# New positions for early loads and conversions, and identity products in PE's early gaps, in a three-phase fp32 attention-and-MLP kernel

## The chip, the cores and the metric

The kernel runs on one core of a Trainium2 chip. The metric is the device time of one execution in microseconds (us), reported as the median of several executions. Each execution also has a span (first to last instruction on the core) and a mean granted clock of PE, the matmul engine. The time was 1.8 to 2.2 us longer than the span in the executions that have both, 1.9 on average. The profile names the engines PE (matmul), PEld (PE's loading of the stationary operand), DVE (vector), ACT (scalar), POOL (general purpose) and SP, which here issues the loads and stores (DMA).

## The reference, cut to what matters

```python
kv  = np.einsum('bhsd,bhse->bhde', k, v)        # batch 8, heads 8, 576 tokens, 64
out = np.einsum('bhsd,bhde->bhse', q, kv)
x   = out / sqrt(mean(out*out, -1) + 1e-6) * g_norm      # -> 4608 x 512
h   = x @ w_in                                   # 512 -> 2048
g   = np.maximum(h, 0) + np.log1p(np.exp(-np.abs(h)))    # softplus
y   = g @ w_out                                  # 2048 -> 512
```

All is fp32, except that the weights arrive as float64 and are converted on the chip.

## The kernel before

Each fp32 operand is split into high and low parts, and a network product is three products of parts that accumulate in one bank. The hidden width is cut into 16 pieces in three phases of 4, 6 and 6; each phase passes over 12 blocks of 384 tokens, so there are 192 steps. A step is 12 products of the first layer and 9 of the second. Phase 0 also computes the attention, interleaved with its steps. Below, a *batch* is one of the eight of the attention.

The order of instructions on each engine is not written by hand. The program lists tasks with a duration, predecessors, buffers and a *position*, and a small planner in the program plays them through and emits them in the order of their planned start. Where several tasks are ready it takes the one with the lowest position:

```python
first = min(at for at, _ in options)
at, t = min(((at, t) for at, t in options if at <= first + self.SOON),
            key=lambda o: (o[1].pos, o[0]))
```

On the chip only the order survives, together with the waits for data and buffers.

```python
rings = dict(xv=2, gv=3, g=2, raw=2, ..., kvt=6, q=2, ..., h=2, o=2, tp=1, s0=1, s1=1, s2=1)
...
# K of two heads lands interleaved, in pieces of 64 floats; V lands in runs of 256 floats
for h in range(2):
    nc.sync.dma_start(out=x[:, h::2], in_=src[:, h])
...
nc.tensor.matmul(kv[:, i if tail else p], lhsT=l, rhs=r, ...)      # a "K and V group" is 4 of these; the profile counts each twice (x8)
...
# a part of a weight is made by PE, with the identity
nc.tensor.matmul(y, lhsT=ident_r, rhs=dst.tile[:, 0], start=True, stop=False)
nc.tensor.matmul(y, lhsT=minus_r, rhs=dst.tile[:, 1], start=False, stop=True)
```

The ring `kvt` has six places, one of which is held for a long time by another tile. A third pair of K and V tiles therefore has to wait until the first group of products has freed its places.

Of the kernel before, what the change touches and what calls it, by code (L numbers as in the profile page):

```python
# [18 lines left out]
P = 128  # L19
# [6 lines left out]
class Slot:  # L26


    def __init__(self, ring):
        self.ring, self.readers, self.place, self.tile = ring, 0, None, None  # L30
# [9 lines left out]
class Plan:  # L40
# [2 lines left out]


    HANDOVER = {"PE": 250, "ACT": 120, "DVE": 120, "POOL": 150, "SP": 0}
    SOON = 150

    def __init__(self, rings):
        self.tasks = []
        self.rings = rings  # L50

    def slot(self, ring):
        return Slot(ring)

    def add(self, engine, ns, run, after=(), pos=0.0, take=(), give=(), size=0, behind=None):
        t = Task(engine, ns, run, [a for a in after if a is not None], pos, list(take), list(give), size)
        for s in t.give:
            s.readers += 1
        self.tasks.append(t)
        t.behind = behind  # L60
        return t

    def order(self):
        waiting = {id(t): sum(1 for a in t.after) for t in self.tasks}
        users = {}
        for t in self.tasks:
            for a in t.after:
                users.setdefault(id(a), []).append(t)
        ready = {}
        for t in self.tasks:  # L70
            if not waiting[id(t)]:
                t.ready = 0
                ready.setdefault(t.engine, []).append(t)
        free = {r: [(0, i) for i in range(n)] for r, n in self.rings.items()}
        engine_free = {"PE": 0, "ACT": 0, "DVE": 0, "POOL": 0, "SP": 0}
        dma_free = 0
        last_read = {}
        done = []
        while len(done) < len(self.tasks):
            best = None  # L80
            for engine, tasks in ready.items():
                options = []
                for t in tasks:
                    at = max(engine_free[engine], t.ready)
                    if t.size:
                        at = max(at, dma_free - 2500)
                    for s in t.take:
                        if not free[s.ring]:
                            break
                        at = max(at, min(free[s.ring])[0])  # L90
                    else:
                        options.append((at, t))
                if not options:
                    continue
                first = min(at for at, _ in options)
                at, t = min(((at, t) for at, t in options if at <= first + self.SOON),
                            key=lambda o: (o[1].pos, o[0]))
                if best is None or at < best[0]:
                    best = (at, t)
            if best is None:  # L100
                raise RuntimeError("the plan is stuck at " + str([(e, t.pos, [s.ring for s in t.take if not free[s.ring]]) for e, ts in ready.items() for t in ts][:20]))
            at, t = best
            ready[t.engine].remove(t)
            for s in t.take:
                place = min(free[s.ring])
                free[s.ring].remove(place)
                s.place = place[1]
            t.start = at
            engine_free[t.engine] = at + t.ns
            t.end = at + t.ns + self.HANDOVER[t.engine]  # L110
            if t.size:
                dma_free = max(dma_free, at + t.ns) + t.size
                t.end = dma_free + 2000
            for s in t.give:
                s.readers -= 1
                last_read[id(s)] = max(last_read.get(id(s), 0), t.end)
                if not s.readers:
                    free[s.ring].append((last_read[id(s)], s.place))
            for u in users.get(id(t), ()):
                waiting[id(u)] -= 1  # L120
                if not waiting[id(u)]:
                    u.ready = max(a.end for a in u.after)
                    ready.setdefault(u.engine, []).append(u)
            done.append(t)
        return sorted(done, key=lambda t: t.start)
# [3 lines left out]
def kernel(  # L129
# [24 lines left out]
    nc = tc.nc  # L154
# [7 lines left out]
    TB = NT // P  # L162
    n_blocks = n_tokens // NT
    n_tiles = n_tokens // P
    PHASES = [range(0, 4), range(4, 10), range(10, 16)]
    PLACES = 8
    LAST = len(PHASES) - 1

    P0 = [-61.0, -9.7, -13.3, -2.2, -4.6, 5.5, -46.9, 0.2, -37.5, -33.8, -28.2, -10.7, -14.2, -13.7, 28.3, -2.7, 1.0, -9.0, 6.5, 7.0, 7.0, 20.0, -0.5, 2.5]
    CONVERT, FETCH, EARLY = P0[:8], P0[8:16], P0[16:]  # L170
    AT_ONCE = 2 * TB

# [6 lines left out]
    ident_r = const.tile([P, P], F32R, name="ident_r")  # L179
# [13 lines left out]
                 h=2, o=2, tp=1, s0=1, s1=1, s2=1)  # L193
    rings.update({f"w{i}_{c}": 1 for i in range(2) for c in range(PLACES)})
    PS = {"h", "o", "tp", "s0", "s1", "s2"}
    plan = Plan(rings)
    slot, add = plan.slot, plan.add

    def new(s, shape, dtype=F32):
        pool = ps if s.ring in PS else sb  # L200
        s.tile = pool.tile(shape, dtype, tag=f"{s.ring}_{s.place}", name=f"{s.ring}_{s.place}")
        return s.tile
# [8 lines left out]
    first_step = {}  # L211
# [163 lines left out]
    x_there = {}  # L375
# [143 lines left out]
            split(0, t, xg, a, pos + 0.5)  # L519

    def x_again(ph, t):
        pos = first_step[ph, t // TB] - 4 + 0.5 * (t % TB)
        xt = slot("xt")
        ld = add("SP", 350, lambda: nc.sync.dma_start(out=new(xt, [P, KD, P]).rearrange("p a t -> p (a t)"), in_=xd[t]),
                 [x_there[t]], pos - 1, [xt], [], 900, behind=first_step[ph, t // TB] - 5)
        split(ph, t, xt, ld, pos)


    part = {}
    scale_done = []  # L530
    mm1s = {}

    def step(s):
# [38 lines left out]
        for i in range(TB):  # L572
            last = c == cs[-1]
            a2 = add("PE", 700, lambda i=i: mm2(i), [a] + factors_done[1, c] + [mm2s.get(i)], s + 1.5,
                     [mine[i]] if c == cs[0] else [],
                     [gv] + ([w_out] if s == last_step[c] else []))
            mm2s[i] = a2
            if last:
                leave(ph, n * TB + i, mine[i], a2, s + 1.5)
# [3 lines left out]
    def leave(ph, t, bank, done, pos):  # L583

        ot = slot("xg" if ph == 0 else ("qT", "x", "q")[t % TB] if ph == LAST else "qT")
        if ph == 0:
            a = add("ACT", 600, lambda: nc.scalar.activation(new(ot, [P, d_model]), bank.tile, func=AF.Copy, scale=1.0 + E),
                    [done], pos, [ot], [bank])
        else:
            pt = slot("kvt")  # L590
            ld = add("SP", 350, lambda: nc.sync.dma_start(out=new(pt, [P, d_model]), in_=part[ph - 1, t][0]),
                     [part[ph - 1, t][1]], pos - 3, [pt], [], 900, behind=int(pos) - 4)
            a = add("DVE", 700, lambda: nc.vector.scalar_tensor_tensor(  # L593
                out=new(ot, [P, d_model]), in0=bank.tile, scalar=(scale if ph == LAST else 1.0 + E), in1=pt.tile,
                op0=ALU.mult, op1=ALU.add), [done, ld] + (scale_done if ph == LAST else []), pos, [ot], [bank, pt])
        dst = out[t * P:(t + 1) * P] if ph == LAST else dram.tile([P, d_model], F32, name=f"part{ph}_{t}")
        st = add("SP", 350, lambda: nc.sync.dma_start(out=dst, in_=ot.tile), [a], pos, [], [ot], 900)
        part[ph, t] = dst, st
# [24 lines left out]
    for x in kv_diag + tails:  # L623
        nc.vector.memset(x, 0.0)

    EACH = (first_step[PHASES[1][0]] - 9) / len(PHASES[1])
    for c in range(KF):
        for j in (2 * c, 2 * c + 1):
            if c in PHASES[0]:
                pos = CONVERT[j]  # L630
            elif c in PHASES[1]:
                pos = 5.0 + EACH * (c - PHASES[1][0] + 0.5 * (j % 2))
            else:
                pos = first_step[PHASES[2][0]] - 64.0 + 9 * (c - PHASES[2][0]) + 4.5 * (j % 2)
            weight(j, pos, FETCH[j] if c in PHASES[0] else pos)
    for b in range(B):
        kv_of(b)
# [3 lines left out]
    for ph in range(len(PHASES)):  # L641
        for n in range(n_blocks):
            for t in range(n * TB, (n + 1) * TB):
                if ph or t >= AT_ONCE:
                    x_again(ph, t)
# [4 lines left out]
    for t in plan.tasks:  # L650
        if t.behind is not None and t.behind >= 0:
            t.after.append(mm1s[t.behind])
    for t in plan.order():
        t.run()

# [29 lines left out]
```

## Time and profile before

| | kernel before |
|---|---|
| time, first set | 940.6 us median of 6 (939.86 to 943.16) |
| span of the profiled execution | 935.2 us (time 937.08 us) |
| PE idle time before the first network product | 16.8 us |
| first network product starts (timeline view) | 44.72 us |
| PE idle time from there to its last product | 0 |
| after PE's last product | 3.7 us |

The lines are in the prediction. Two habits help in reading them. First, the "time" of a kernel whose main engine is never idle after some moment is that moment, plus a constant; so only the moment is worth study. Second, a PE product's own duration tells whether the clock was up: eight identical attention products take about 2.05 us at the low clock and 0.89 at the full one. (The timeline view gives a group up to 0.2 us more than the chain does, since it includes the pipeline's end.)

### The profile page before, as it was taken

Reading aid. Unit: us, or ns where it says so; the run is one execution under the profiler, and the core shown is the slowest. Engines: PE = TensorE matmul, PEld = TensorE weight load, DVE = VectorE, ACT = ScalarE, POOL = GpSimd, SP = SyncE. Lnnn points to the kernel's source line nnn. Section 1 sums busy time; section 2 is a strip of 40 time slices with the busy share of each in tenths; the row PEclk is TensorE's granted clock in tenths of the full one; section 3 lists DMA queues with packets and bytes.
Section 4 is the critical chain, followed back from the end, with each engine's and each line's share of the span. In section 5 each row is a group of like instructions: output and inputs, shape, how many; then the busy total and the mean of one; then the engine's idle time right before and its main releaser. Section 6 shows DMA issues by size and latency. Waiting matters only on the chain.

```text
span 935.2 us, 13489 instructions
## 1 busy us (share of the span) xinstructions
PE 914.7 (98%) x4978; PEld 831.9 (89%) x4978; DVE 598.0 (64%) x1045; ACT 446.4 (48%) x871; POOL 66.2 (7%) x42
## 2 busy tenths in 40 slices
PE   4899999999999999999999999999999999999998
PEld 3799899999999899899989989899999999999997
DVE  7988876767777747676676665586455454444543
ACT  5877675756666635444344343374323333232331
POOL 0331212212222000000000000000000000000000
PEclk9999999999999999999999999999999999999999
DMA  9999677776554333434343332343232323322221
GB/s 248 251 261 265 198 219 219 221 210 192 172 193 141 119 124 125 146 124 134 137 134 106 122 139 100 135 145 102 102 102 102 102 102 102 101 91 75 91 82 69
DMA packets 148673, 135.63 MB, mean 145 GB/s; under 512 B 86400, under 2 KB 102784, under 8 KB 148608
## 3 DMA queue, kind: packets, MB, share of 16 engines
q1 hardware_dynamic: 148448, 134.78, 47.2%
q8 instruction: 39, 0.64, 0.3%
q14 instruction: 26, 0.21, 0.1%
q10 hardware_dynamic: 160, 0.00, 0.0%
HBM read 93.85 MB, written 40.89 MB: 144 GB/s over the span
## 4 chain that ended last, share of the span: by engine, by line
PE 96%; DMA 2%; SPq 0%; ACT 0%; issue 0%; DVE 0%; ACTq 0%
PE h L546 43%; PE s L553 43%; PE o L460 4%; PE o L484 3%; PE tp L500 2%; PE tp L478 2%; DMA q<-in_q_dram 1%; DMA kvt<-in_v_dram 1%; SPq L444 0%; PE s L484 0%; PE h L345 0%; PE h L344 0%; SPq L250 0%; DVE q L593 0%; ACT x L508 0%
## 5 line engine op out<-in xcount | busy, mean ns | idle before, releaser
L553 PE MATMUL s<-w,gv 128*128 128x512 f32 x1728 | 437.7, 396 | 0.0
L546 PE MATMUL h<-xv,w 128*128 128x384 f32 x2304 | 435.8, 337 | 0.0
L546 PEld LDWEIGHTS h<-xv,w 128*128 128x128 f32 x2304 | 405.4, 188 | 14.0 <-issue 0.2
L553 PEld LDWEIGHTS s<-w,gv 128*128 128x128 f32 x1728 | 318.3, 188 | 57.5 <-issue 0.3
L566 ACT ACTIVATE g<-h 128x384 f32<-128x384 f32 x192 | 94.3, 491 | 403.6 <-PE h L546 400.2
L557 DVE TENSOR_TENSOR gv<-g,gv 128x384 fp32r<-128x384 f32 x192 | 106.8, 556 | 173.3 <-ACT gv L568 172.9
L561 DVE SCALAR_TENSOR_TENSOR gv<-gv 128x384 fp32r<-128x384 f32 x192 | 107.0, 557 | 5.5
L568 ACT ACTIVATE gv<-g 128x384 fp32r<-128x384 f32 x192 | 100.7, 525 | 5.9 <-PE s L553 0.9
L401 DVE TENSOR_TENSOR xv<-xt,xv 128x512 fp32r<-128x512 f32 x102 | 70.2, 688 | 49.6 <-ACT xv L398 49.0
L492 POOL TENSOR_TENSOR r<-r,half 128x8 f32<-128x8 f32 x36 | 65.5, 1819 | 228.4 <-DVE r L489 228.4
L404 DVE SCALAR_TENSOR_TENSOR xv<-xv 128x512 fp32r<-128x512 f32 x108 | 74.5, 690 | 2.7
L398 ACT ACTIVATE xv<-xt 128x512 fp32r<-128x512 f32 x102 | 63.6, 623 | 11.0 <-DMA xt<-x 10.9
L460 PE MATMUL o<-kvt,kvt 128*128 128x128 f32 x256 | 36.9, 292 | 11.4 <-DMA kvt<-in_v_dram 10.9
L460 PEld LDWEIGHTS o<-kvt,kvt 128*128 128x128 f32 x256 | 35.1, 206 | 12.9 <-issue 12.0
L593 DVE SCALAR_TENSOR_TENSOR qT<-s,kvt 128x512 f32<-128x512 f32 x36 | 24.8, 688 | 28.5 <-PE s L553 25.9
L484 PE MATMUL o<-kv_diag,qT 128*128 128x128 f32 (+1 forms) x296 | 36.9, 276 | 0.0
L484 PEld LDWEIGHTS o<-kv_diag,qT 128*128 128x128 f32 (+1 forms) x296 | 34.6, 179 | 1.1 <-issue 0.8
L514 ACT ACTIVATE xg<-tp,g_col 128x512 f32<-128x512 f32 x36 | 24.7, 687 | 11.2 <-PE tp L500 11.0
L488 DVE TENSOR_REDUCE r<-x 128x8 f32<-128x512 f32 x36 | 24.6, 683 | 6.3 <-ACT x L508 6.0
L495 DVE TENSOR_TENSOR x<-o,r 128x512 f32<-128x512 f32 x33 | 22.7, 688 | 9.0 <-POOL r L492 8.6
L593 DVE SCALAR_TENSOR_TENSOR qT<-s,scale,kvt 128x512 f32<-128x512 f32 x12 | 9.0, 751 | 29.5 <-PE s L553 29.5
L503 ACT COPY qT<-tp 128x512 f32<-128x512 f32 x36 | 21.0, 583 | 12.7 <-PE tp L478 12.6
(66 smaller groups left out, 484.9 us busy)
## 6 DMA issues: line engine op xcount, KB each, us to landing
xt<-x SPq DMA_DIRECT2D x102, 256.0 KB, 3.3
kvt<-part SPq DMA_DIRECT2D x72, 256.0 KB, 4.4
x<-xg SPq DMA_DIRECT2D x36, 256.0 KB, 2.6
part<-xg SPq DMA_DIRECT2D x36, 256.0 KB, 2.5
part<-qT SPq DMA_DIRECT2D x36, 256.0 KB, 2.5
raw<-in_moe_w_in_dram SPq DMA_DIRECT2D x16, 512.0 KB, 5.2
raw<-in_moe_w_out_dram SPq DMA_DIRECT2D x16, 512.0 KB, 4.8
kvt<-in_k_dram SPq DMA_DIRECT2D x64, 128.0 KB, 4.0
```

The source lines that it names most:

```text
L398: nc.scalar.activation(cols(0, F32R), x.tile, func=AF.Copy, scale=DOWN)
L401: nc.vector.tensor_tensor(out=cols(1, F32R), in0=x.tile, in1=cols(0), op=ALU.subtract)
L404: nc.vector.scalar_tensor_tensor(out=cols(2, F32R), in0=cols(1), scalar=-RADIX, in1=cols(0), op0=ALU.mult, op1=ALU.add)
L460: nc.tensor.matmul(kv[:, i if tail else p], lhsT=l, rhs=r, start=(p == 0 and i == 0), stop=tail, skip_group_check=True)
L484: nc.tensor.matmul(pairs(y[r0:r0 + n], p), lhsT=qT.tile[:, p, r0:r0 + n], rhs=kv_diag[b % 2][:, p], start=(p == 0), stop=True, skip_group_ ...
L492: nc.gpsimd.tensor_tensor(out=r.tile, in0=r.tile, in1=half, op=ALU.pow)
L546: nc.tensor.matmul(hp, lhsT=w_in.tile[:, i, kd * P:(kd + 1) * P], rhs=xv.tile[:, i, kd], start=(m == 0), stop=(m == 3 * KD - 1))
L553: nc.tensor.matmul(mine[i].tile, lhsT=gv.tile[:, m, i * P:(i + 1) * P], rhs=w_out.tile[:, m], start=(c == cs[0] and m == 0), stop=(c == cs ...
L557: nc.vector.tensor_tensor(out=gv.tile[:, 1], in0=g.tile, in1=gv.tile.bitcast(F32)[:, 0], op=ALU.subtract)
L561: nc.vector.scalar_tensor_tensor(out=gv.tile[:, 2], in0=f32[:, 1], scalar=-RADIX, in1=f32[:, 0], op0=ALU.mult, op1=ALU.add)
L566: a = add("ACT", 490, lambda: nc.scalar.activation(new(g, [P, NT]), h.tile, func=AF.Softplus, scale=1.0 + E), [a], s, [g], [h])
L568: a = add("ACT", 530, lambda: nc.scalar.activation(new(gv, [P, 3, NT], F32R)[:, 0], g.tile, func=AF.Copy, scale=DOWN), [a], s, [gv])
```

## The change

The intent is to fill PE's early gaps with products of the identity whose results nobody reads, so that its clock stays up, and to replace hand-picked positions by ones found by playing the order through with varied landing times of the loads. The planner puts a filler wherever a 400 ns product ends before PE's next real task would start, from 4 us of planned time until the first network product. The diff, cut to its core (the bookkeeping of the planner's loop is left out):

```diff
@@ class Plan
+    BEGIN = 4000
...
+        self.spare = None
...
+                if engine == "PE" and self.spare and self.spare[-1].start is None:
+                    ring, run, ns, _ = self.spare
+                    begin = max(engine_free["PE"], self.BEGIN, min(free[ring])[0] if free[ring] else at)
+                    if begin + ns <= at:
+                        s = Slot(ring)
+                        at, t = begin, Task("PE", ns, lambda s=s: run(s), [], 0.0, [s], [s], 0)
+                        s.readers = 1
...
-    P0 = [-61.0, -9.7, -13.3, -2.2, -4.6, 5.5, -46.9, 0.2, -37.5, -33.8, -28.2, -10.7, -14.2, -13.7, 28.3, -2.7, 1.0, -9.0, 6.5, 7.0, 7.0, 20.0, -0.5, 2.5]
+    P0 = [-57.5, -0.2, -24.8, -1.2, -4.6, 5.5, -63.4, 1.2, -34.0, -33.3, -32.7, -11.2, -17.2, -25.2, 23.8, -3.7,
+          1.0, -9.5, 6.5, 7.0, 7.0, 24.5, -0.5, 2.5, 2.5, 8.5, -9.5, 5, 9, 67.5, 8]
     CONVERT, FETCH, EARLY = P0[:8], P0[8:16], P0[16:]
...
-        pos = first_step[ph, t // TB] - 4 + 0.5 * (t % TB)
+        pos = first_step[ph, t // TB] - EARLY[8] + 0.5 * (t % TB)          # conversion of reloaded x
-                 [x_there[t]], pos - 1, [xt], [], 900, behind=...)
+                 [x_there[t]], pos - EARLY[9], [xt], [], 900, behind=...)  # its reload
...
-                     [part[ph - 1, t][1]], pos - 3, [pt], [], 900, behind=...)
+                     [part[ph - 1, t][1]], pos - EARLY[10], [pt], [], 900, behind=...)
...
-    EACH = (first_step[PHASES[1][0]] - 9) / len(PHASES[1])
+    EACH = (first_step[PHASES[1][0]] - EARLY[12]) / len(PHASES[1])
...
-                pos = 5.0 + EACH * (c - PHASES[1][0] + 0.5 * (j % 2))
+                pos = EARLY[11] + EACH * (c - PHASES[1][0] + 0.5 * (j % 2))
...
-                pos = first_step[PHASES[2][0]] - 64.0 + 9 * (c - PHASES[2][0]) + 4.5 * (j % 2)
+                pos = first_step[PHASES[2][0]] - EARLY[13] + EARLY[14] * (c - PHASES[2][0]) + EARLY[14] / 2 * (j % 2)
...
+    def warm(s):
+        nc.tensor.matmul(new(s, [P, 4, P]), lhsT=ident_r, rhs=ident_r.unsqueeze(1).to_broadcast([P, 4, P]),
+                         start=True, stop=True)
+
+    plan.spare = ("h", warm, 400, mm1s[0])
```

More of the change, by code (lines that the diff above doesn't have):

```diff
@@ L77, in order @@
         last_read = {}
-        done = []
-        while len(done) < len(self.tasks):
+        done, left = [], len(self.tasks)
+        while left:
             best = None
@@ L102, in order @@
             at, t = best
-            ready[t.engine].remove(t)
+            if t in ready[t.engine]:
+                ready[t.engine].remove(t)
+                left -= 1
             for s in t.take:
@@ L521, in x_again @@
     def x_again(ph, t):
-        pos = first_step[ph, t // TB] - 4 + 0.5 * (t % TB)
+        pos = first_step[ph, t // TB] - EARLY[8] + 0.5 * (t % TB)
         xt = slot("xt")
         ld = add("SP", 350, lambda: nc.sync.dma_start(out=new(xt, [P, KD, P]).rearrange("p a t -> p (a t)"), in_=xd[t]),
-                 [x_there[t]], pos - 1, [xt], [], 900, behind=first_step[ph, t // TB] - 5)
+                 [x_there[t]], pos - EARLY[9], [xt], [], 900, behind=first_step[ph, t // TB] - 5)
         split(ph, t, xt, ld, pos)
@@ L591, in leave @@
             ld = add("SP", 350, lambda: nc.sync.dma_start(out=new(pt, [P, d_model]), in_=part[ph - 1, t][0]),
-                     [part[ph - 1, t][1]], pos - 3, [pt], [], 900, behind=int(pos) - 4)
+                     [part[ph - 1, t][1]], pos - EARLY[10], [pt], [], 900, behind=int(pos) - 4)
             a = add("DVE", 700, lambda: nc.vector.scalar_tensor_tensor(
```

## The prediction

> **What bounds the kernel now.** I read the page's busy shares first, then the windows view over the stages, then the chain that ended last.
>
> ```profile
> PE 914.7 (98%) x4978; PEld 831.9 (89%) x4978; DVE 598.0 (64%) x1045; ACT 446.4 (48%) x871; POOL 66.2 (7%) x42
> ```
>
> PE is busy 914.7 of 935.2 us, so 20.5 us is all the idle time there is. The windows view (start:end, length, then busy time of PE, PEld, DVE, ACT, POOL, granted clock, DMA share, GB/s) says where it lies:
>
> ```profile
> 0.00:8.70 8.70, 0.00 (x0) 0.01 (x1) 5.85 (x14) 4.78 (x8) 0.70 (x6) 1.00 0.75 211
> 8.70:20.60 11.90, 9.20 (x45) 8.21 (x45) 8.55 (x15) 6.38 (x13) 0.00 (x0) 0.86 1.18 272
> 20.60:44.70 24.10, 18.66 (x142) 15.70 (x143) 21.84 (x40) 20.45 (x39) 7.18 (x4) 1.00 1.15 254
> 44.70:330.00 285.30, 285.30 (x1773) 263.38 (x1772) 213.59 (x383) 188.94 (x368) 58.28 (x32) 1.00 0.69 199
> 330.00:931.60 601.60, 601.54 (x3024) 544.59 (x3022) 347.38 (x595) 225.85 (x445) 0.00 (x0) 1.00 0.33 111
> 931.60:935.20 3.60, 0.00 (x0) 0.00 (x0) 0.73 (x2) 0.00 (x0) 0.00 (x0) 0.81 0.58 219
> ```
>
> Before 44.7 us PE idles 44.7 - 9.20 - 18.66 = 16.8 us; after 931.6 us the last output leaves in 3.6 us; between them PE is never idle. Busy is not peak, so I also asked the chain between those two times whether any piece of it is stretched: grouped by kind, every product there costs the same (first product of the network 175 ns, second 231 ns, attention products 110 ns); the only longer pieces are one group of twelve at 2.33 and one at 2.21 us instead of 2.10, 0.34 us together. So after the first product of the network, which starts at 44.96 us in the chain, there is nothing to win: 931.55 - 44.96 = 886.6 us of pure PE work. The time is this start, plus 886.6, plus 3.6.
>
> What sets the start is read from the chain in order of time (start, length, what; cuts marked):
>
> ```profile
> 3.15 5.44 DMA kvt<-in_v_dram
> 8.58 0.14 issue
> 8.72 2.06 PE o L460 x8
> 10.78 0.02 issue
> 10.80 4.24 DMA kvt<-in_v_dram
> ...
> 17.25 1.98 PE o L460 x8
> ...
> 19.69 0.90 PE o L460 x8
> ...
> 29.87 4.57 DMA q<-in_q_dram
> 34.44 0.14 issue
> 34.58 0.64 PE tp L478 x4
> 35.22 0.02 issue
> 35.24 5.96 DMA q<-in_q_dram
> ```
>
> It is a ladder of loads: a product frees a buffer, the freed buffer lets the next load be issued, that load lands 4 to 6 us later. The loads are slow because the DMA engines are full: share 1.18 and 1.15 at 272 and 254 GB/s from 8.7 to 44.7 us. DVE (21.84 of 24.1) and ACT (20.45) are nearly full there as well.
>
> **What the Trainium skill says.** "TensorE: Matmul & The Clock Gate", Part 1 (the HAM clock gate): PE runs at half clock until about 3.4 us of sustained activity, and falls back after an idle window. The trace agrees in the durations: eight identical attention products took 2.06 us at 8.72 and 1.98 us at 17.25, but 0.90 at 19.69 and 0.89 everywhere later. Its clock column shows only the second of these (0.86 mean in that stage, and 0.50 between 16 and 18 us in a finer view), so for the first I believe the durations. The same page gives 427 ns cold and 216 ns warm for a product with 512 columns; the before trace has 230 ns warm for such a product (the pairs with the identity that divide a weight). "DMA: Bandwidth & Descriptors", Specifications: line rate needs 512 B or more per descriptor, and HBM gives a core about 358 GB/s. The page of the profile counts 86,400 of 148,673 packets under 512 B, which fits the early rate of 250 to 270 GB/s. In "Queues, rings and completion order" it has every DMA from one issuer share the same 16 engines: so reordering loads lets one land earlier only by making another later. The landing times here (4 to 6 us under load against 2.0 to 2.6 for the late stores) agree.
>
> **The change part by part.** The real work is the same: 939 PE rows before, and 980 after with 41 identity products of 512 columns added. All 41 stand ahead of the first network product, so none can cost anything later except by delaying that start.
>
> Comparing orders: the 37 PE rows of real work before the first network product are the same rows in the same order. The DVE order is the same for its first 83 rows; ACT's differs only in rows 6 to 9 (the squaring for the second weight waits until the first weight's overflow check is through). On the DMA queue, the first K and V loads move ahead of the second 512 KB weight load, and one K tail load moves behind the next two; from the thirteenth row to the eightieth that order is then unchanged. Nearly all the moved positions act past the first network product, on DVE and ACT conversions and reloads.
>
> 1. First K and V earlier. 512 KB less in front of them at 250 to 270 GB/s is 2.0 us: they should land near 6.7 instead of 8.6 us. The third V load is issued when the first products have freed its buffer (10.80 us, at the end of those products). With a start near 6.9 and 1.0 to 2.0 us of products, the buffer frees by 8 to 9 us; the queue reaches that load at about 9 us. So it is issued some 1.8 us earlier. But the engines are full, and the second weight's bytes now lie among them: I keep about half, 0.9 us.
> 2. Warm clock. Groups at 17.25 and the first ones before it cost 1.64 + 1.98 against 2 x 0.89 warm: 1.8 us of excess. The load of the fourth V lands at about 17.2 in any case if the DMA rate stays, so only the fourth group's own excess, 1.98 - 0.89 = 1.1 us, is on the path.
> 3. Cost of the fillers. Each about 0.23 us warm (0.43 cold, an estimate from the clock page): 6 cold ones from 1.6 us (the identity is ready at 1.57) end at 4.2, before any data. The other 35 are 35 x 0.23 = 8 us, against 16.8 - 8.7 = 8.1 us of measured idle time after the first data. So they fit only just, and not gap by gap: four stand before a transpose of q where the trace has 0.65 us of waiting, so 0.3 us may be added there, and two more sites may add as much. I charge 0.5 us, since a late transpose also delays the next q load.
> 4. Afterwards. There is no slack to win, so new positions of conversions and reloads can only lose or break even; that they were chosen for varying landings argues for zero. DVE has 213.6 of 285.3 us busy and ACT 188.9 up to 330 us, so room remains. A small wait somewhere, 0.2 us, is charged.
>
> Sum: -0.9 - 1.1 + 0.5 + 0.2 = -1.3 us in the profiled span. The timed runs (940.79 median) are 3.7 us longer than the profiled execution (937.08), and that difference cannot be read here. If part of it comes from landings which vary between runs, an order chosen for varied landings gets some back: I add -1.0 us as a guess. 940.8 - 1.3 - 1.0 = 938.5 us.
>
> **Rivals.** (a) DMA hides everything. The start at 44.96 us is set by the bytes ahead of the last needed q tile, and these are the same. For it: share above 1.1 throughout, and the unchanged order of loads from the thirteenth row on. Against it: the rungs of the ladder where a freed buffer issues the load (10.80, 28.17, 35.24 us). Then 940 to 941. (b) Fillers get in the way. PE keeps program order, so when data come earlier than planned the fillers stand in front of real products, and each costs 0.23 us or twice that if the clock stays low; with waits between fillers for one of the two banks they may cost more. Fully exposed, the 19 fillers behind the first batch's K and V products would be 4.4 us: 943 to 945. Against it: the gaps they were put in are mostly seen in the trace. (c) The whole ladder moves: each rung inherits the earlier buffer, and PE idle falls by 4 to 6 us. For it: four rungs pass through PE. Against it: full DMA, DVE and ACT. Then 935 to 936. (d) A new wait in the first stage past the start, because conversions of weights come later than the products that need them: PE would show idle time between 45 and 330 us. Then up to 945.
>
> **Range and chances.** Two per cent is 18.8 us, more than all the idle time before the start (16.8), of which 6 to 7 us is unavoidable first landing. So faster by over 2% is almost excluded. Slower by over 2% needs more than all 41 fillers exposed (41 x 0.23 = 9.4 us) plus a new stall. Rival (a) is the likeliest of the others, then (c), then (b). The range 934.8 to 942.0 covers (a) and (c) and half of (b).
>
> **What would show it.** Right: first attention products near 7 us; eight of them at 0.9 us each group from about 10 us on; the first network product at 43 to 44.5 us; no PE idle time between it and the last product; PE's busy time up by about 8 to 11 us while the idle time before the start falls by as much. Wrong: the start unchanged although PE is warm (a); transposes of q beginning later than the landing, behind identity products (b); a start before 42 us (c); a wait of PE on a weight's conversion after 45 us (d). If timed runs fall by much more than the profile's start moves, the gain came from the runs that no profile shows.

## The result, and the profile after

| set of runs | before, mean (runs) | changed, mean (runs) | ratio (95% interval) |
|---|---|---|---|
| first | 941.03 (6) | 938.97 (6) | 0.9978 (0.9965 to 0.9992) |
| second | 940.52 (11) | 939.38 (5) | 0.9990 (0.9975 to 1.0004) |
| fourth | 939.93 (11) | 939.89 (6) | 0.9998 (0.9979 to 1.0016) |

The result of the first set, which the prediction was about, is 938.95 us median (938.22 to 940.17) against 940.6. The second and fourth sets were run later, next to the experiments. The third set, on another chip, has experiments and the kernel before, but not the changed kernel. Over the three sets of the table the gain is between nothing and 2 us. A gain of about 1 us is likely, but only the first set's interval excludes that there is none.

The surprise is in the profile. The changed kernel's profiled execution has a span of 936.5 us, 1.3 us *longer* than the 935.2 of before, where the prediction's sum had it 1.3 us shorter. First the busy line of the page and the windows view (start:end, length, then busy time of PE, PEld, DVE, ACT, POOL, granted clock, DMA share, GB/s):

```profile
PE 925.1 (99%) x5019; PEld 837.3 (89%) x5019; DVE 601.5 (64%) x1045; ACT 449.3 (48%) x871; POOL 66.9 (7%) x42
```

```profile
0.00:8.70 8.70, 4.56 (x14) 3.32 (x15) 5.84 (x14) 3.64 (x6) 0.70 (x6) 1.00 0.77 224
8.70:20.60 11.90, 10.68 (x56) 7.89 (x55) 8.57 (x15) 7.53 (x15) 0.00 (x0) 1.00 1.17 272
20.60:44.70 24.10, 21.94 (x153) 17.28 (x152) 20.81 (x38) 19.64 (x38) 7.15 (x4) 1.00 0.95 238
44.70:330.00 285.30, 285.12 (x1774) 263.01 (x1773) 213.68 (x385) 188.99 (x368) 59.06 (x32) 1.00 0.69 200
```

PE is 10.4 us busier, and in the three early rows it has filled most of its idle time: 44.7 - 4.56 - 10.68 - 21.94 = 7.5 us are left of 16.8. DMA share and rate, the last two columns, hardly moved in the first two rows; in the third they fell from 1.15 to 0.95 and from 254 to 238 GB/s, so the engines are less full there than the prediction took them to be. The 0.18 us that are missing in the last row are a transpose that waited for DVE at 165.6 us. Now the chain that ended last, in order of time (start, length, what; L668 is the filler, L472 a K and V group):

```profile
2.61 4.32 DMA kvt<-in_v_dram
6.93 0.14 issue
7.06 2.05 PE o L472 x8
9.11 2.47 PE h L668 x7
11.58 0.89 PE o L472 x8
...
12.50 5.33 DMA kvt<-in_v_dram
17.83 0.04 issue
17.87 1.16 PE o L472 x8
...
19.49 0.91 PE o L472 x8
...
34.55 5.95 DMA raw<-in_moe_w_out_dram
...
45.86 2.09 PE h L558 x12
```

The first K and V did land earlier, as predicted (6.93 instead of 8.58 us). The fourth group ran at the full clock, 1.16 us instead of 1.98. The first batch's last group ended at 20.40 instead of 20.59. But the first network product starts later: 45.86 instead of 44.96 in this view (45.61 and 44.72 in the timeline). So the profile says that the change lost 0.9 us ahead of the start, while the timed runs say that it won. The loss lies between the end of the first batch's groups and the start: 25.5 us instead of 24.4. The chain passes there through the load of a second-layer weight, for which DVE waits (34.55); it does so in five of the eight traces that have the new order of loads with K in its old form, and in none of the four with the old order. Why that load binds there is not shown. The experiments are about this contradiction.

### The profile page after: what moved, and what is told of

It reads as the page before. It is cut to its first block, busy times and chain, and to the rows that moved or that the text cites. A ratio compares the mean times of both kernels' runs of the same rounds, so it can differ in the third digit from the quotient of the medians.

```text
span 936.5 us, 13571 instructions
## 1 busy us (share of the span) xinstructions
PE 925.1 (99%) x5019; PEld 837.3 (89%) x5019; DVE 601.5 (64%) x1045; ACT 449.3 (48%) x871; POOL 66.9 (7%) x42
## 2 busy tenths in 40 slices
DMA packets 148673, 135.63 MB, mean 145 GB/s; under 512 B 86400, under 2 KB 102784, under 8 KB 148608
## 4 chain that ended last, share of the span: by engine, by line
PE 95%; DMA 2%; DVE 1%; ACT 1%; issue 0%; SPq 0%; ACTq 0%
PE h L558 43%; PE s L565 42%; PE o L472 3%; PE o L496 3%; PE tp L512 2%; PE tp L490 1%; DMA kvt<-in_v_dram 1%; DMA raw<-in_moe_w_out_dram 1%; DMA part<-xg 0%; PE s L496 0%; PE h L668 0%; DVE xv L413 0%; PE h L357 0%; DVE xv L416 0%; SPq L456 0%
## 5 line engine op out<-in xcount | busy, mean ns | idle before, releaser
L413 DVE TENSOR_TENSOR xv<-xt,xv 128x512 fp32r<-128x512 f32 x102 | 70.1, 687 | 17.8 <-ACT xv L410 17.5
L472 PE MATMUL o<-kvt,kvt 128*128 128x128 f32 x256 | 35.0, 281 | 3.7 <-DMA kvt<-in_v_dram 3.7
L472 PEld LDWEIGHTS o<-kvt,kvt 128*128 128x128 f32 x256 | 33.4, 195 | 5.8 <-issue 3.2
```

The lines of the kernel that those rows point to most:

```text
L413: nc.vector.tensor_tensor(out=cols(1, F32R), in0=x.tile, in1=cols(0), op=ALU.subtract)
L472: nc.tensor.matmul(kv[:, i if tail else p], lhsT=l, rhs=r, start=(p == 0 and i == 0), stop=tail, skip_group_check=True)
```

## The experiments

Two theories were on the table. **W**: the identity products hold PE's clock up, and that is the whole gain; the first trace of the kernel before was an unusually quick execution. **P**: the new positions are the gain. For both I could keep the order of all real instructions fixed: with fillers switched off in the planner, the order of every engine's other instructions came out unchanged, for the new positions and for the old ones. So the change separates into two clean factors.

Below, *start* is the first network product in the timeline view, and *the batch ends* with the first batch's last K and V group. Each profile is one execution; the times are medians, and a mean is called one.

### The kernel before, again

No edit.

> The kernel before, unchanged, for a second trace and the spread of its runs. The first trace had a span of 935.2 us, while its timed runs (940.6 us median) must have spans near 938.7. If the first trace was a lucky execution, this one has a span of 937.5 to 940 and the first network product starts at 47 to 49 us instead of 44.96 with the work behind it still 886.6 us. Rival: the start is near 45 us again and the extra 3 us are waits of PE behind the start. Time ratio 1.000 within 0.1%.

Measured: 940.57 us median (939.86 to 941.51, 5 runs), ratio 1.000 (0.9985 to 1.0015), span of the trace 939.6 us. Its start is 48.87 us, 4.15 us later than in the first trace, and the work behind it is 887.1 us with 0.06 us of idle time, nearly as before (886.8). So the start alone differs between two executions of the same kernel. Two lines of PE's timeline (start, length, operation, and in brackets the idle time ahead) show one reason:

```profile
39.25 1.09 PE L478 MATMUL tp<-ident_r,q 128*128 128x128 f32 x4 [1.52 <-ACT qT L503]
40.13 1.91 PE L484 MATMUL o<-kv_diag,qT 128*128 128x128 f32 x8
```

The same eight products took 1.06 us in the first trace. The clock had fallen again, late in the start, after a few waits of 0.6 to 1.5 us. In this trace the first four groups were also slow, up to 22.17 us, where the first trace recovered at 19.7. The first trace was the lucky one: of the 36 later executions of the kernel before, the shortest span is 935.8 us.

### Identity products with the old positions

```diff
-    P0 = [-57.5, -0.2, -24.8, ... 2.5, 8.5, -9.5, 5, 9, 67.5, 8]
+    P0 = [-61.0, -9.7, -13.3, ... 4, 1, 3, 5.0, 9, 64.0, 9]     # the old values
```

> The old positions with the 41 identity products (every real instruction in the order of the kernel before). Theory W (the gain is the warm clock and the regular start it gives): 938.5 to 939.5 us, nearly all of the 1.7 us gain. Theory P (the gain is the positions): 940 to 942 us, no gain or a loss of up to 1 us from products standing in front of real work.

Measured: 939.57 us median (938.08 to 940.29, 5 runs), ratio 0.9990 (0.9975 to 1.0004), the same ratio as the whole change beside it; start 46.21, batch end 20.3 us. This is what W expects, though the interval alone does not exclude that nothing changed. With the later repeat below, the mean is 939.24 us in 11 runs against 940.22 in the 22 of the kernel before beside them: 1.0 us less, and by my working from these runs the 95% interval is about 0.2 to 1.8.

### The new positions without identity products

```diff
-    plan.spare = ("h", warm, 400, mm1s[0])
+    plan.spare = None
```

> The new positions without identity products (every real instruction in the order of the changed kernel). Theory W: 940 to 941 us, no gain; the first groups of attention products cold at about 2 us each. Theory P: 938 to 939.5 us, nearly all of the gain.

Measured: 940.76 us median (939.21 to 945.03, 6 runs), ratio 1.0007 (0.9988 to 1.0026). No gain is seen, which speaks against P, but the interval is wide enough to hide one of 1 us (and one run of 945.03 us widens it); the tiny products below settle it. The chain of its trace shows what the products had been doing:

```profile
10.46 2.06 PE o L472 x8
...
12.54 4.98 DMA kvt<-in_v_dram
...
17.57 2.08 PE o L472 x8
...
20.49 1.72 PE o L472 x8
```

Compare this with the chain of the changed kernel. Without fillers the second group starts 1.1 us earlier, as soon as its V has landed, but takes 2.06 us; with them it waits behind seven fillers and then takes 0.89. Both end at the same time (12.52 and 12.47), and the next load, which needs the freed buffer, is issued at 12.54 and 12.50 us. At that rung the fillers cost exactly what they bring. The gain comes after: the fourth group and the last one are fast, and the batch ends at 20.40 instead of 22.21 us. The recorded clock of this window (the third column from the end) reads 1.00 in both traces, although the groups differ by a factor of two. Without fillers:

```profile
8.70:20.60 11.90, 8.20 (x32) 6.84 (x31) 8.55 (x15) 6.63 (x14) 0.00 (x0) 1.00 1.18 268
```

### The changed kernel, again

No edit.

> The changed kernel, unchanged, for a second trace and the spread: 938.5 to 939.5 us, ratio 0.998 to before; span 936.4 to 938, first network product between 45 and 47 us, no PE idle time behind it. Its runs should scatter less than those of the kernel before (0.5 us rather than 1.2 us standard deviation).

Measured: 939.37 us median (937.97 to 940.48, 5 runs), ratio 0.9990 (0.9975 to 1.0004), span 938.6. The start is 47.19 us, slightly beyond what I expected, since the first V landed at 8.61 us in this execution instead of 6.93; the span is beyond it too (936.4 to 938), and behind the start PE idles 0.46 us where I expected none. The scatter of its runs is 0.84 us here (standard deviation) where I expected 0.5, against 1.22 for the kernel before.

### Tiny identity products

```diff
-        nc.tensor.matmul(new(s, [P, 4, P]), lhsT=ident_r, rhs=ident_r.unsqueeze(1).to_broadcast([P, 4, P]),
+        nc.tensor.matmul(new(s, [P, 4, P])[:, 0, :8], lhsT=ident_r, rhs=ident_r[:, :8],
```

> The changed kernel with each of the 41 identity products cut from 512 columns to 8: the same places, banks and waits, but hardly any array work. Theory W (only the activity of the array counts): the K and V groups run cold again at about 2.05 us, the recorded clock is below 1.0 in several runs, and the time is that of the positions alone, 940.2 to 941.2 us (ratio 0.9995 to 1.0010). Rival S (the extra instructions help in another way, by spacing or by the banks they take, or the new positions need them): 938.5 to 939.5 us, ratio 0.998 to 0.999.

Measured: 940.7 us median (940.16 to 942.87, 5 runs), ratio 1.0017 (1.0005 to 1.0030); so even a little slower than the kernel before of its set (939.41 mean), and beyond the ratio of 1.0010 that W allowed. The kernel of the same set with all fillers and six more (below) had a mean of 939.55, against 941.04 here. PE's timeline:

```profile
6.93 2.05 PE L472 MATMUL o<-kvt,kvt 128*128 128x128 f32 x8 [3.85 <-DMA kvt<-in_v_dram]
17.75 2.08 PE L472 MATMUL o<-kvt,kvt 128*128 128x128 f32 x8
```

All four groups are cold. The same 41 instructions in the same places, with the same banks and waits, do not warm the groups when they hardly use the array: it is the activity that counts. The rival that instructions help by spacing is out, and so is P: positions without activity bring no gain.

### Only the first 22 fillers, and only the last 19

```diff
+        warmed.append(s)
+        if len(warmed) > 22:        # the other kernel: <= 22
+            return
```

> The changed kernel with only the first 22 identity products, those ahead of the fifth K and V group of the first batch. Theory W1 (the early warm-up is the whole gain): K and V groups warm from the second on, 938.7 to 939.5 us. Theory W2 (the later 19 are needed against a fallback of the clock between 20 and 45 us): some runs with a recorded clock of 0.993 to 0.997 and times above 941, median 939.7 to 940.5.

> The changed kernel with only the last 19 identity products (from the first batch's last K and V group on). Theory W1: the first batch's groups cold as in the positions alone, its end at about 22.2 us instead of 20.4, median 940 to 941 us. Theory W2: the recorded clock stays at 0.998 to 1.0 and no run is over 941; median 939.3 to 940.

Measured: 940.39 us median (939.27 to 941.87, 5 runs) with the early ones, ratio 1.0011 (0.9999 to 1.0024); 940.82 (940.19 to 941.2, 5 runs) with the late ones, ratio 1.0015 (1.0001 to 1.0029). The kernel before of this set was at 939.41 mean, lower than in the other sets, so I read these by their traces. With the early ones alone the batch ends at 20.8 us, but then:

```profile
37.09 1.09 PE L490 MATMUL tp<-ident_r,q 128*128 128x128 f32 x4 [1.02 <-DMA q<-in_q_dram]
39.76 1.92 PE L496 MATMUL o<-kv_diag,qT 128*128 128x128 f32 x8
```

This is the fallback that the second trace of the kernel before also had; the start is 48.70 us. With the late ones alone three of the first four groups are cold (2.04, 2.05, 1.13 and 2.08 us), the batch ends at about 21.5 us, and the start is 46.97 us with no fallback behind 22 us. For the late ones W2 expected no run over 941 us; there were two (941.05 and 941.2). So W1 alone and W2 alone both look too little: in these two traces each half guards its own stretch. In time the two halves are 0.9 and 1.2 us slower than the full fillers of this set (939.55 mean), which is about the scatter of five runs.

### Twelve identity products ahead of the first group instead of six

```diff
-    BEGIN = 4000
+    BEGIN = 1600
```

> The changed kernel with six more identity products ahead of the first K and V group (12 instead of 6), so that PE is active from 1.6 us until about 6.9 us. If the first group ran cold only because PE idled from 4.5 to 7.1 us, it now runs in 0.9 to 1.2 us instead of 2.05, the seven products behind it in 1.7 us instead of 2.5, and the load which waits for the second group is issued 1.5 us earlier; time 937.5 to 939 us if the DMA lets it land earlier, 938.7 to 939.5 (no change) if the DMA rate binds.

Measured: 939.56 us median (937.85 to 940.65, 5 runs), ratio 1.0002 (0.9989 to 1.0014). The first group is warm now, as expected, and nothing comes of it:

```profile
7.74 1.13 PE L472 MATMUL o<-kvt,kvt 128*128 128x128 f32 x8 [0.64 <-DMA kvt<-in_v_dram]
18.09 1.16 PE L472 MATMUL o<-kvt,kvt 128*128 128x128 f32 x8 [1.37 <-DMA kvt<-in_v_dram]
```

The load ahead of the fourth group was not issued 1.5 us earlier, as I had expected, but at 12.58 us, as in the changed kernel (12.50). The second group could begin only at 11.01 us, when its loads had landed. By then the first two groups were done (12.14 us), and SP was still issuing the loads ahead of this one in its queue, until 12.48. PE's speed is no longer what sets this rung; the loads are.

### The whole change and the fillers alone, on another occasion

No new edits.

> The changed kernel once more, because the kernel before was itself 1.1 us faster on the chip of the last set (939.4 mean) than on the one before (940.5). If the gain is real on every chip, the ratio is 0.998 to 0.999 again; if on this chip the kernel before keeps its clock up by itself (recorded clocks of 0.996 to 0.998 and none of 0.993), the ratio is 0.999 to 1.0005 and its own runs are 938.5 to 939.5 us as on both occasions before.

> The old positions with the identity products, once more: as the changed kernel within 0.5 us (theory W: the products are the whole effect), 938.5 to 939.7 us; if the positions bring something that the first comparison hid, 0.7 us or more slower than the changed kernel of this set.

Measured: the changed kernel 939.78 us median (938.69 to 941.75, 6 runs), ratio 0.9998 (0.9979 to 1.0016); the fillers at the old positions 939.11 (938.71 to 939.74, 6 runs), ratio 0.9989 (0.9972 to 1.0006). The fillers alone do at least as well as the whole change in both sets. My reading that the kernel before would hold its clock here did not hold: it had runs from 937.68 to 943.72, the slowest at a recorded clock of 0.990 and the next at 0.993, and the ratio was near 1 all the same. The trace of the changed kernel shows that fillers are no guarantee. After a wait of 1.75 us for a load, its fourth group was cold:

```profile
18.99 2.02 PE L472 MATMUL o<-kvt,kvt 128*128 128x128 f32 x8 [1.75 <-DMA kvt<-in_v_dram]
```

The start was 48.13 us in that execution.

### K of the first two batches in longer runs

If loads set the start, faster loads should move it. The next two kernels test that; they are further changes on top of this one, not parts of it. K lands in pieces of 64 floats because two heads are interleaved for one 128 x 128 product. This version lets each head land in runs of 256 floats, and makes one 64 x 64 product per head. The result is correct.

```diff
-                        nc.sync.dma_start(out=x[:, h::2], in_=src[:, h])
+                        nc.sync.dma_start(out=x[:, 4 * h:4 * h + 4] if b < 2 else x[:, h::2], in_=src[:, h])
...
+                    if b < 2 and not tail:
+                        for h in range(2):
+                            nc.tensor.matmul(kv[h * D:(h + 1) * D, p, h], lhsT=ks.tile[:, 4 * h + i],
+                                             rhs=vs.tile[:, 4 * h + i], start=(p == 0 and i == 0), stop=False,
+                                             skip_group_check=True)
+                        continue
```

> The changed kernel with K of the first two batches landing in runs of 1 KB instead of 256 bytes, and therefore two products of 64 x 64 per 128 x 128 product (the result is right). If the descriptor-bound DMA rate sets the first network product's start, the start moves from 45.6-47.2 to 42-45 us and the time to 936 to 938 us. If the dependent chain through ACT and DVE sets it, start and time stay within 0.7 us; if the doubled products cost more than 0.3 us per group, the time rises by up to 1 us.

Measured: 936.7 us median (935.76 to 939.26, 6 runs), ratio 0.9966 (0.9947 to 0.9985), span 934.9. This beats both kernels: 3.0 us below the changed kernel of the same set (936.87 against 939.89 mean), and 3.1 below the kernel before. PE's timeline:

```profile
11.55 0.69 PE L474 MATMUL o<-kvt,kvt 128*64 128x64 f32 x16
17.46 0.69 PE L474 MATMUL o<-kvt,kvt 128*64 128x64 f32 x16 [0.98 <-DMA kvt<-in_v_dram]
44.05 2.33 PE L564 MATMUL h<-xv,w 128*128 128x384 f32 x12
```

The start is at 44.05 us, as expected if the loads set it (42 to 45). The doubled products did not cost more, as I had feared: sixteen of them take 0.69 us here, where eight of the larger ones take 1.05 in this view. So two things became faster at once, the loads and the products, and this run alone can't say which moved the start.

### K and q in contiguous runs, with a wrong result

```diff
-                        nc.sync.dma_start(out=x[:, h::2], in_=src[:, h])
+                        nc.sync.dma_start(out=x[:, 4 * h:4 * h + 4], in_=src[:, h])
...
-                nc.sync.dma_start(out=x[r0:r0 + n], in_=src[b, :, s0:s0 + n].rearrange("h s d -> s h d"))
+                nc.sync.dma_start(out=x[r0:r0 + n].rearrange("s h d -> s (h d)"), in_=...)   # as many floats, contiguous
```

> Wrong result on purpose: K and q of all batches land in contiguous runs (1 and 2 KB) with the same bytes and the same number of transfers, every instruction otherwise as in the changed kernel. Packets under 512 bytes fall from 86,400 to below 20,000. If the DMA rate with short runs sets the start: first network product at 38 to 43 us, time 932 to 936 us. If not: within 1 us of the changed kernel.

Measured: 936.67 us median (936.5 to 937.34, 6 runs), ratio 0.9965 (0.9947 to 0.9984), start 43.31 us; the result is wrong. The page's line on packets, a row of the windows view, and the start in the chain:

```profile
DMA packets 91841, 135.63 MB, mean 145 GB/s; under 512 B 16768, under 2 KB 41344, under 8 KB 91776
```

```profile
8.70:20.60 11.90, 11.84 (x61) 8.98 (x61) 9.70 (x18) 8.69 (x17) 0.00 (x0) 0.86 0.97 295
```

```profile
43.56 2.09 PE h L560 x12
```

Here PE's products are those of the changed kernel, and only the loads are different. So faster loads by themselves bring some 3 us. That is less than I expected from removing four fifths of the short packets (932 to 936 us, start at 38 to 43), and the start is within the trace-to-trace scatter of the version above. The rest of the start is held by something else: in this trace the chain from the batch's end (19.23 us) to the first network product (43.56) passes through PE, ACT and DVE alone and through no load, with DVE 21.6 and ACT 20.0 of 23.5 us busy. How much of the gain of the correct version is due to its shorter products stays open.

## Why the prediction was right or wrong

**The time was right, the sum behind it only in part.** 938.5 us was predicted and 938.95 measured. But the sum started from the first trace, and this trace was not typical; and one of its three large terms was a guess. So the agreement is in good part luck. What was forecast for the profile failed: a first network product at 43 to 44.5 us came at 45.61, a span 1.3 us shorter came out 1.3 longer, and PE waited 0.18 us behind the start where no wait was expected. The prediction's last sentence covers this case: when the timed runs fall by more than the profile's start moves, the gain lies in runs that no profile shows.

**"The time is this start, plus 886.6, plus 3.6": right.** In the traces of the kernel before, the changed one and the nine others of the experiments, the work behind the start lies between 886.8 and 888.3 us, and the starts between 43.31 and 48.87 us explain the rest of the spans.

**Step 1, "first K and V earlier", 0.9 us: the mechanism was right, the worth was not shown.** In the eight traces that have the new order and K in its old form, the first group started between 6.87 and 7.74 us, except once at 8.74; in the four with the old order it was 8.72 to 8.92. But the new positions without fillers brought nothing: ratio 1.0007, and 1.0017 with tiny ones. The load whose early issue I had counted on, the one ahead of the third group, was issued earlier (9.14 instead of 10.80 us), but the fourth group's V still landed at 17.5 to 19.0 us in the seven traces of the new order (K in its old form) whose chain passes it, while in the first trace of before that group had started at 17.25. What the first landing wins is lost by the fourth.

**Step 2, "warm clock", 1.1 us: right in mechanism, and it is the gain that the runs show.** The fourth group fell from 1.98 to 1.16 us in the first pair of traces (0.8), and in the comparison of the same order with and without fillers the batch ends 1.8 us earlier. The prediction did not have the later fall of the clock, near 40 us, which two traces without the later fillers show. Measured in time, fillers brought 1.1 us in the second set and 0.8 in the fourth at the old positions, and 1.6 us at the new ones (941.02 against 939.38 mean; one run of 945.03 makes up half of it) and 1.5 in the third set (tiny products 941.04, full ones with six more 939.55).

**Step 3, fillers charged with 0.5 us: a charge exists, but elsewhere.** At the transpose of q behind four fillers, where the prediction put it, PE still waited 0.71 us for the load. The charge falls where seven fillers stand ahead of the second group, 1.1 us, and is given back there by the faster group. PE's busy time rose by 10.4 us, inside the stated 8 to 11.

**Step 4, 0.2 us of new waits after the start: right in kind, a little small.** Three traces of the changed kernel show 0.18, 0.46 and 0.63 us of idle time there; two of the kernel before show 0 and 0.06.

**"I add -1.0 us as a guess": without it the forecast would have been 939.5, and its stated cause was not borne out.** I put it to positions chosen for varied landings; the positions alone brought nothing. The runs point to the clock. The recorded mean clock of an execution tells roughly how often it fell back: one stretch of 3.4 us at half rate (the window that the Trainium skill gives in "TensorE: Matmul & The Clock Gate", Part 1) takes 1.7 of about 938 us, so 0.998 is one such stretch, 0.996 two, 0.993 four. That is an estimate; the traces agree, since a stretch of 10 us with one fallback reads 0.83. Two things blur it: a fall behind PE's last product counts too and costs nothing (0.81 over the last 3.6 us of the first trace), and a cold start can leave no mark (1.00 in the trace without fillers, whose four groups were cold). The 36 executions of the kernel before that were recorded with their clock sort as follows:

| recorded clock | kernel before: runs, mean us | changed kernel: runs, mean us |
|---|---|---|
| 0.998 and above | 10, 939.09 | 17, 939.42 |
| 0.996 and 0.997 | 20, 940.00 | none |
| 0.995 and below | 6, 941.94 | none |

Executions of the kernel before with few recorded falls are as fast as the changed kernel, and the order is the same within each set; in the changed kernel no execution has a record below 0.998. This sorting is a correlation, and it is not strict: two of the eleven runs of the fillers at the old positions have 0.996 and 0.997 and took 939.12 and 938.71 us. That activity is what warms the groups is shown by the tiny products; that both halves are needed is suggested by the two kernels with half of them (one trace each).

**The step that failed:** taking 44.96 us as *the* start of the kernel before, and taking from it 0.9 us for the first K and V and 1.1 for the fourth group. It was the start of one quick execution; the next trace had 49.12 in the same view, with the same work behind it. And the 0.9 us never reached the start, because the fourth V landed no earlier. Working it out from the mean of the 36 runs, 940.07 - 1.9 - 887.0 - 3.7, gives about 47.5 us as an estimate; for the 17 runs of the changed kernel 939.42 - 1.9 - 887.6 - 3.7 gives 46.2. So the start moved about 1.3 us earlier on average, and some 0.6 us more work and waiting behind it gave part of that back. The prediction had the warning in hand (timed runs 3.7 us longer than the profiled one) and could not read it. One reading in it was selective: among the late stores beside the 2.0 to 2.6 us there is also a third of the output's that took 4.1.

**The rivals.** (a), that DMA hides everything, is the better half of the truth: making the first group fast changed nothing, and making the loads faster did. (b) is seen at one rung and repaid. (c), the whole ladder, did not come: the fourth V landed no earlier, and behind it the chain also passes through ACT and DVE. (d) is seen at half a microsecond, but not for its reason: PE waited for a result of DVE (0.18 and 0.45 us) and for a load of V (0.55), not for a weight's conversion.

**Open:** why the effect was 2.1 us in the first set and nothing in the fourth, beyond scatter; one of the fourth set's executions shows a fallback in spite of the fillers. And whether the positions cost something by themselves: both comparisons without active fillers are on the slow side (0.5 and 1.6 us), one of them beyond its interval, and the two with half of the fillers are 1.0 and 1.3 us slower than the kernel before of their set. With all fillers the two sets of positions take the same time within the scatter (939.24 in 11 runs at the old ones, 939.66 in 11 beside them at the new).

## What to carry to other kernels

When the main engine is never idle after some moment, time equals that moment plus a constant; take several traces before trusting where the moment is, because the start of a kernel varies more than its body. Keeping PE active through its start was worth about 1 of 940 us here, where its clock otherwise falls in some executions, but only until the loads take over as the limit; then look at how short the runs of the loads are. Sorting timed runs by their recorded clock costs nothing and can point to a cause that no single trace shows; an experiment then has to confirm it.

## What the Trainium skill lacked or had wrong

- "TensorE: Matmul & The Clock Gate", Part 1, lets the clock fall after an idle window of about 3.4 us, and advises against gaps of that length. Further on it describes falls from frequent short idle times, without saying how short. Here, once up, it fell with no gap longer than 1.75 us: groups of 2.02 us after a wait of 1.75 us in the changed kernel, and of 1.92 us after waits of 1.68 and 1.02 us with the early fillers alone. A stretch that is partly idle is enough.
- The same page warns that recorded clock events are unreliable, but not in which way. Here the record leaves out the low clock at the very start: the profile's clock column reads 1.00 from 8.7 to 20.6 us in the trace without fillers, where groups took 2.05 us instead of 0.89. Durations of equal products are the safer sign.
- No page that I read says how little a filler may do: 41 products of 8 columns left every early group at 2.05 us, 41 of 512 columns brought most to 1.05 to 1.16.
- No page that I read has a figure for fp32 products of half the columns and half the stationary width: sixteen of 64 x 64 took 0.69 us where eight of 128 x 128 took 1.05 us.
- "DMA: Bandwidth & Descriptors", Specifications, asks for 512 B per descriptor. That is not wrong, but what it is worth had to be measured. Here, cutting the packets below 512 B from 86,400 to 16,768 raised the rate between 8.7 and 20.6 us from 272 GB/s (241 and 256 in the other two traces of the changed kernel) to 295, at a DMA share of 0.97 instead of 1.17, and brought about 3 of 940 us; behind the batch's end the chain then passed through no load.
